# Sines before copies, one evacuation for the taps, and even-phase products kept in place, in a gated SSM and token-MLP kernel

## The chip, the cores and the metric

The kernel runs on one core of one Trainium2 chip. Its time is the device time of one execution, in microseconds (us). Six runs of the kernel before give a median of 189.79 us (188.96 to 190.0). One more execution was taken with the hardware profiler on; its own time was 191.53 us, of which 189.7 us are the span that the profile shows.

The engines are named as in the profile: PE is TensorE (PEld its weight loads), ACT is ScalarE, DVE is VectorE, POOL is GpSimd, and SP issues most of the DMAs. A `q` behind the name means that engine's queue.

## What is computed

Two branches share the input x = A_q (2048 x 640, bf16) and are mixed by a gate for each row. Branch A is a long convolution along the sequence, done by a Fourier transform in the reference. Branch B is an MLP over the sequence after a LayerNorm.

```python
g = sigmoid((x * gate_w).sum(-1, keepdims=True))
# A: k is shifted and weighted by 4 taps, multiplied by v, convolved with ssm_k
k_shift = sum over t of k_pad[:, t:t+S, :] * shift_k[:, 3 - t]
kv = k_shift * v
y = irfft(rfft(kv padded to 2S) * rfft(ssm_k padded to 2S))[:S] + kv * ssm_D
a = q * y
# B: MLP over the sequence axis
h = layernorm(x)
u = gelu(einsum("bsd,sf->bdf", h, w1) + b1)
b = transpose(einsum("bdf,fs->bds", u, w2) + b2)
out = g * a + (1 - g) * b
```

## The kernel before

**The planner.** The body of `_build` does not issue instructions directly. Each helper (`mms` for a group of matmuls, `act`, `tt`, `ts`, `dma`) adds an operation with an engine, a modelled duration, what it reads and writes, and a priority (by default its place in the text; `prio=0` is the most urgent). `_Sched.run` then plays a list schedule through: whenever an engine is free it takes, of the operations whose inputs are ready in the model, the one with the lowest priority number. The order that results is the program order of each engine, and the hardware waits are put in afterwards by `_Tracker` where data demand them. An `after` entry only orders two operations in the plan and makes no hardware wait. A DMA is modelled at 365 GB/s behind all earlier ones, plus 2 us. "QA" is the DMA queue of ScalarE, "SP" that of SyncE; `chain=True` keeps the SP loads in the order of the text.

**PSUM.** Four slots of 128 x 1024 f32. Groups of class "cv" (convolution branch and transposes) may hold three, "mlp" groups two. A group holds its slot from its first matmul to the end of its evacuation. The planner starts the matmuls of a group only when everything that its evacuation depends on is done.

**The stages.**
1. Small loads (D, shift taps, b2, b1), then ssm_k, x, w1, k, v on the SP queue.
2. Cosine and sine tables FTB, one of 1024 columns for each phase p. VectorE makes integer arguments `pint` (a product, an addition, a mask); ScalarE applies Sin. `pint` lies in the ring[1] buffer, which the k loads (`kn`) and one of the turned k buffers (`kp0`) use later. PORD = (0, 2, 1, 3) is the order of the phases.
3. `transp`: TensorE transposes ssm (five blocks db for each half h, eight matmuls each); ScalarE copies them to wT, which lies in C[2].
4. Taps. The loaded taps are rearranged by a VectorE copy ("taps") in `rows`, transposed by small matmuls ("cst"), and copied by ScalarE to `cw`. GpSimd spreads them to KF, which the products with k use as moving operand. `consts` does the same for b2 and b1 (cc).
5. `fwd(srcW(h), ...)`: for each half h and phase p four groups of four matmuls, 64 for each half, evacuated by ScalarE to C[h]. This is called W here. `mixing(C[0], SS, ...)` and `mixing(C[1], C[0], ...)` combine the phases on VectorE.
6. LayerNorm on VectorE (`ln_tile`, `ln_apply`), with the power on GpSimd (`ln_scale`), in two parts: tiles 0 to 7 are applied after the statistics of twelve tiles, the rest later. The first MLP product (m1, 384 matmuls, with a gelu for each of 12 blocks ft) needs the normalised X; its priority is so low that it fills TensorE's gaps.
7. `kv(hk)`: products of KT (k transposed by DMA) with KF, times v, for four blocks; blocks 0, 1 give vkv0 (source A), blocks 2, 3 give kv1 (source B).
8. `fwd_even` and `fwd` for A into C[2], for B into C[3]. Phases 1 and 3 are done by `fwd`, four groups each. Phases 0 and 2 share products: `fwd_even` makes eight groups of two matmuls, evacuates each to 640 columns of a temporary (Th, Ts) and forms slots 0 and 2 of the destination by three VectorE operations over them (two of 1280 columns and one of 2560, called the sums below). The temporary is slots 0 and 1 of C[1] for A and of C[2] for B. `mixing(C[1], C[0])` reads those slots of C[1] until its last operation, and `mixing(C[2], C[1])` those of C[2]. So phases 0 and 2 can be evacuated only after the mixing in question.
9. `mixing(C[2], C[1])`, `mixing_acc(C[3], ...)`, then the products in the spectrum (`cross`, `product`), partly summed by DMAs from GpSimd's queue, `invmix` and `inverse` for two halves, with ScalarE evacuating by the gate gg.
10. The second MLP product (m2, 384 matmuls, 16 groups), also filler, and the sum with branch A; the output is written in nine DMAs.

The gate's products (VectorE: X times gwb, 1280 columns, eight of them) and sums (ScalarE) are further filler between these.

All priorities of mixing C[0] and C[1] are MIXP = 330; the products of kv with v have priority 0.

The two lines that say where even-phase products go:

```python
act(V(Th, Ts * SL + D * pos[(p, kt, c)], [[320, 2], [1, 320]]), two, ACT.Copy, vt=vt, name="Ae")
fwd_even(srcA, 0, C[2], C[1], 0)
```

Of the kernel before, what the change touches and what calls it, by code (L numbers as in the profile page):

```python
# [323 lines left out]
class _Sched:  # L324
# [59 lines left out]
    def run(self):  # L384
# [12 lines left out]
        pend = {e: [] for e in engs}  # L397
        free = {e: 0.0 for e in engs}
        port = {"DVE": 0.0, "POOL": 0.0}
# [13 lines left out]
        n = len(ops)  # L413
# [97 lines left out]
def _build(nc, A_q, A_k, A_v, A_shift_k, A_ssm_k, A_ssm_D, B_x, B_w1, B_b1, B_w2, B_b2, gate_w, out):  # L511
# [10 lines left out]
    with ExitStack() as es:  # L522
# [27 lines left out]
        def base_of(h):  # L550
            return T.mem[h.name][1]
# [43 lines left out]
        ksh = [alloc(f"ksh{i}", [128, 4, D], BF16, at=base_of(GT) + 5120 * (1 + i)) for i in range(2)]  # L595
        rows = alloc("rows", [20, 4, 512], BF16, at=base_of(GT))
        kn = [alloc(f"kn{i}", [128, 4, D], BF16, at=base_of(ring[1]) + 5120 * i) for i in range(2)]
# [116 lines left out]
        def dr(t, off, ap):  # L714
            return bass.AP(tensor=t.tensor, offset=t.offset + off, ap=ap)
# [19 lines left out]
        def x_load(hk):  # L735
            dma(X[:, hk, :, :], dr(A_q, 512 * hk * D, [[4 * D, 128], [1, 4 * D]]), 128 * 5120, chain=True)
# [23 lines left out]
        def small(o, i, nbytes, stream, **kw):  # L760
            dma(o, i, nbytes, stream=stream, **kw)
# [3 lines left out]
        small(Drow[:, :], dr(A_ssm_D, 0, [[0, 1], [1, D]]), 1280, "QA")  # L765
        small(rows[0:20, 0, 0:128], dr(A_shift_k, 0, [[128, 20], [1, 128]]), 5120, "QA")
        small(rows[0:4, 1, :], dr(B_b2, 0, [[512, 4], [1, 512]]), 4096, "QA")
        small(rows[0:12, 2, 0:128], dr(B_b1, 0, [[128, 12], [1, 128]]), 3072, "QA")
        for a, b in SSM0:
            ssm_load(0, a, b)  # L770
        for hk in range(4):
            x_load(hk)
        for a, b in SSM1:
            ssm_load(1, a, b)
# [11 lines left out]
        ts("DVE", ident[:, :], dif[:, :], 0.0, None, ALU.is_equal)  # L786
        memset("POOL", cw[:, :, :], 0.0)
        ro, ri = rows[0:20, 3, :].rearrange("g (j q c) -> g j q c", j=4, q=4), V(rows, 0, [[1, 4], [0, 4], [4, 32]], pn=20)
        SC.add("DVE", 0.6, lambda s: T.op("DVE", lambda e: e.tensor_copy(ro, ri), [ri], [ro]), [ri], [ro], prio=0, name="taps")
        PORD = (0, 2, 1, 3)  # L790
        for p in PORD:
            pv = pint[:, p, :, 1, :]
            tt("DVE", pv, V(acol, p, [[4, 2], [0, 256]]), V(brow, 0, [[0, 2], [1, 256]]), ALU.mult, mode=1)
            ts("DVE", pint[:, p, :, 0, :], pv, 1024.0, None, ALU.add, mode=2)
            pa = pint[:, p, :, :, :].rearrange("q a b c -> q (a b c)")
            ts("DVE", pa, pa, 4095, None, ALU.bitwise_and, mode=2)
            act(FTB[:, p, :, :, :, :].rearrange("q a b c d -> q (a b c d)"), pa, ACT.Sin, bias=cst[:, 0:1],
                scale=-(2.0 * math.pi / 4096.0) * (1.0 - 1e-6), name="sin")
# [39 lines left out]

# [13 lines left out]

        def fwd_even(src, h, dst, Th, Ts):
# [9 lines left out]
            def t4(o, n, dims):  # L863
                return V(Th, Ts * SL + D * o, dims + [[1, n]])
            tt_("DVE", V(dst, 0, [[2 * D, 2], [1, D]]), t4(0, 2 * D, []), t4(2, 2 * D, []), ALU.add)
            tt_("DVE", V(dst, 2 * SL + 2 * D, [[-2 * D, 2], [1, D]]), t4(4, 2 * D, []), t4(6, 2 * D, []), ALU.add)
            tt_("DVE", V(dst, D, [[2 * SL, 2], [2 * D, 2], [1, D]]), t4(0, D, [[4 * D, 2], [D, 2]]), t4(2, D, [[4 * D, 2], [D, 2]]), ALU.subtract)

# [52 lines left out]
        for h in range(2):  # L921
            for db in range(ND):
                transp(h, db)
            if h == 0:
                consts()
            for p in PORD:
                fwd(srcW(h), h, p, C[h], p, 1.0 / 1024.0, "W", (lambda c, k2: False) if h == 0 else (lambda c, k2: c == 1))
            if h == 0:
# [14 lines left out]
                for g0 in KFP:  # L943
                    tt("POOL", KF[:, g0:g0 + 20 // len(KFP), :, :], V(cw, 7 * g0, [[7, 20 // len(KFP)], [1, 7], [0, 32]]), V(m32, 0, [[0, 20 // len(KFP)], [0, 7], [1, 32]]), ALU.mult)
                for hk in range(2):
# [313 lines left out]
```

## Time and profile before

| what | us |
|---|---|
| median of six runs | 189.79 |
| profiled execution, its own time | 191.53 |
| span of the profile | 189.7 |
| first transpose on TensorE | 3.93 |
| first wT copy on ScalarE | 5.04 |
| first W matmul on TensorE | 16.41 |
| last W evacuation, half 0 | 30.16 |
| mixing of C[1] begins on VectorE | 50.39 |
| mixing of C[2] begins on VectorE | 78.79 |
| first inverse begins on TensorE | 158.35 |
| second inverse begins on TensorE | 174.85 |
| last TensorE work ends | 187.04 |

Busy time by stage (us busy in each stretch):

| stretch | PE | DVE | ACT | POOL |
|---|---|---|---|---|
| 0 to 6 | 1.54 | 5.00 | 2.24 | 1.21 |
| 6 to 16.4 | 5.42 | 9.60 | 10.27 | 5.77 |
| 16.4 to 30.2 | 13.79 | 11.21 | 10.36 | 5.69 |
| 30.2 to 50.4 | 19.29 | 16.37 | 18.03 | 14.85 |
| 50.4 to 66.4 | 15.95 | 15.53 | 14.20 | 2.67 |
| 66.4 to 78.8 | 12.30 | 7.48 | 12.40 | 2.43 |
| 78.8 to 98.6 | 18.62 | 19.47 | 18.78 | 0.89 |
| 98.6 to 158.2 | 59.60 | 59.37 | 17.85 | 12.28 |
| 158.2 to 174.8 | 15.59 | 12.99 | 9.00 | 4.80 |
| 174.8 to 189.7 | 12.20 | 11.69 | 6.34 | 0.00 |

A busy TensorE is not TensorE at its best: matmuls are pipelined, and a slow one counts as busy all the while. In a line of a timeline the columns are: start, length, engine, line of the code, operation, destination and source with their shapes, number of instructions merged, and in brackets the idle time before and what ended it. In the chain of waits the columns are start, length and what the chain ran through. Most operations carry the line of a helper (L667 for every ACT evacuation, L623 for every two-input VectorE operation, L293 for every matmul), so the names of the tiles tell them apart; buffer numbers are left out, so "C" is any of C[0] to C[3].

### The profile page before, as it was taken

What the parts mean: (1) busy time and instruction counts of PE and PEld (TensorE: products, weight loads), DVE (VectorE), ACT (ScalarE), POOL (GpSimd) and SP (SyncE); (2) the same over time, 40 slices, a digit from 0 to 9 for tenths busy, and PEclk for the clock granted to TensorE, in tenths of its full rate; (3) what the DMA queues carried; (4) which work ended last, traced back from release to release, by engine and by line L of the source; (5) the groups of instructions that cost most, each with busy time, mean ns of one, the idle gap of its engine ahead of it and who ended that gap; (6) DMA issues with size and microseconds to landing.
All of it is one profiled execution on the core that took longest, in us unless ns stands there. A gap on an engine that the chain in (4) does not pass through costs nothing.

```text
span 189.7 us, 3316 instructions
## 1 busy us (share of the span) xinstructions
PE 174.3 (92%) x1374; PEld 130.1 (69%) x1374; DVE 168.7 (89%) x199; ACT 119.5 (63%) x180; POOL 50.6 (27%) x41
## 2 busy tenths in 40 slices
PE   2746999989999999999979999999999999997994
PEld 1523668756877786767747777888888887675673
DVE  7899795999399963999999999999999999849984
ACT  2996789699997999999798111322313134553660
POOL 2079404999000550000011530200205050342000
PEclk9999999999999999999999999999999999999999
DMA  5999999899990799990799699957949999999453
GB/s 173 377 412 369 386 199 238 345 416 207 200 352 24 182 211 230 232 202 0 137 222 271 108 192 159 340 98 211 313 90 284 271 190 243 275 196 226 105 207 138
DMA packets 38206, 42.85 MB, mean 226 GB/s; under 512 B 15787, under 2 KB 31280, under 8 KB 38192
## 3 DMA queue, kind: packets, MB, share of 16 engines
q1 hardware_dynamic: 33200, 32.15, 56.9%
q0 software_dynamic: 4928, 10.49, 31.1%
q8 instruction: 10, 0.16, 0.3%
q14 instruction: 4, 0.03, 0.1%
q10 hardware_dynamic: 64, 0.01, 0.0%
HBM read 25.87 MB, written 2.62 MB: 150 GB/s over the span
## 4 chain that ended last, share of the span: by engine, by line
PE 80%; ACT 15%; DMA 2%; issue 1%; DVE 0%
PE pp L293 80%; ACT C L667 4%; ACT wT L667 3%; ACT FTB L667 3%; ACT ksh L667 2%; DMA ssm<-in_A_ssm_k_dram 2%; ACT L667 1%; ACT GT L667 1%; ACT O L667 0%; ACT cw L667 0%; DVE O L679 0%; ACT gth L667 0%
## 5 line engine op out<-in xcount | busy, mean ns | idle before, releaser
L623 DVE TENSOR_TENSOR C<-C 128x2560 bf16<-128x2560 bf16 (+2 forms) x34 | 52.2, 1564 | 7.3 <-ACT C L667 7.2
L293 PE MATMUL pp<-X,ring 128*128 128x320 bf16 x384 | 55.4, 299 | 1.5 <-ACT GT L667 1.2
L293 PE MATMUL pp<-GT,W 128*128 128x320 bf16 x384 | 52.8, 299 | 0.0
L293 PEld LDWEIGHTS pp<-GT,W 128*128 128x128 bf16 x384 | 43.4, 113 | 8.9 <-ACT cgb L667 0.2
L293 PEld LDWEIGHTS pp<-X,ring 128*128 128x128 bf16 x384 | 37.2, 98 | 16.5 <-issue 1.9
L667 ACT ACTIVATE C<-pp 128x640 bf16<-128x640 f32 x64 | 40.5, 717 | 6.5 <-PE pp L293 6.4
L667 ACT ACTIVATE O<-pp,c,omg 128x640 bf16<-128x640 f32 x15 | 13.3, 885 | 34.7 <-PE pp L293 34.7
L293 PE MATMUL pp<-wT,FTB 128*128 128x320 bf16 x128 | 21.8, 329 | 2.2 <-ACT wT L667 1.4
L262 POOL DMA_DIRECT2D C<-q_hi x6 | 5.9, 984 | 54.5 <-DVE C L623 27.6
L293 PEld LDWEIGHTS pp<-wT,FTB 128*128 128x128 bf16 x128 | 13.0, 107 | 9.8 <-ACT wT L667 1.5
L262 POOL DMA_DIRECT2D C<-C x8 | 9.9, 1360 | 34.0 <-DVE C L623 33.8
L667 ACT ACTIVATE GT<-pp,cc 128x640 bf16<-128x640 f32 x12 | 9.5, 791 | 13.1 <-PE pp L293 12.9
L667 ACT ACTIVATE cgb<-pp,gg 128x640 bf16<-128x640 f32 x16 | 12.7, 793 | 6.9 <-PE pp L293 5.4
L293 PE MATMUL pp<-C,FTB 128*128 128x320 bf16 x96 | 13.6, 299 | 1.1 <-ACT O L667 1.1
L996 POOL COPY KT<-KT 128x20 bf16<-128x20 bf16 x1 | 14.0, 13956 | 2.3 <-DMA KT<-kp 2.3
L623 DVE TENSOR_TENSOR tm<-C,C 128x2560 bf16<-128x2560 bf16 (+1 forms) x7 | 14.4, 2057 | 0.0
L899 DVE BATCH_NORM_STATS2 stats<-X 128x6 f32<-128x320 bf16 x32 | 13.4, 461 | 0.8 <-DMA X<-in_A_q_dram 0.8
L623 DVE TENSOR_TENSOR SS<-C 128x2560 bf16<-128x2560 bf16 x8 | 11.6, 1486 | 2.0 <-DMA C<-C 1.8
L293 PEld LDWEIGHTS pp<-C,FTB 128*128 128x128 bf16 x96 | 8.9, 98 | 5.4 <-ACT O L667 1.6
L623 DVE TENSOR_TENSOR C<-tm 128x2560 bf16<-128x2560 bf16 (+1 forms) x10 | 12.0, 1219 | 0.0
L667 ACT ACTIVATE gq<-gq 128x640 bf16<-128x640 bf16 x16 | 11.8, 748 | 0.0
L293 PE MATMUL pp<-ident,ssm 128*128 128x128 bf16 x80 | 8.4, 270 | 3.7 <-DMA ssm<-in_A_ssm_k_dram 2.6
(69 smaller groups left out, 192.9 us busy)
## 6 DMA issues: line engine op xcount, KB each, us to landing
ring<-in_B_w_dram SPq DMA_DIRECT2D x12, 512.0 KB, 11.0
W<-in_B_w_dram SPq DMA_DIRECT2D x8, 768.0 KB, 7.2
C<-C POOLq DMA_DIRECT2D x8, 640.0 KB, 10.7
X<-in_A_q_dram SPq DMA_DIRECT2D x4, 640.0 KB, 8.5
kn<-in_A_k_dram SPq DMA_DIRECT2D x4, 640.0 KB, 8.4
out_dram<-O SPq DMA_DIRECT2D x7, 320.0 KB, 2.8
ssm<-in_A_ssm_k_dram SPq DMA_DIRECT2D x3, 512.0 KB, 5.8
vkv<-in_A_v_dram SPq DMA_DIRECT2D x2, 640.0 KB, 5.0
```

What stands on the lines that cost most here:

```text
L262: ins = engobj.dma_start(out_ap, in_ap, accum_op=ALU.add, max_dma_last_dim=2560)
L293: ins = self.nc.tensor.matmul(ps_ap, lhsT=lhsT, rhs=rhs, start=start, stop=stop, skip_group_check=True)
L623: o_ = SC.add(eng, d, lambda s: T.op(eng, lambda e: e.tensor_tensor(o, a, b, op), [a, b], [o]), [a, b], [o], prio=prio, name="tt")
L667: return T.op("ACT", lambda e: e.activation(o, src, func, **kw), rr + [src], ww)
L899: ops.append(SC.add("DVE", 0.38, (lambda o, i: lambda s: T.op("DVE", lambda e: e.bn_stats(o, i), [i], [o]))(o, i), [i], [o]))
L996: SC.add("POOL", 0.3, lambda s: T.op("POOL", lambda e: e.tensor_copy(KT[1][:, :, 15:16], KT[0][:, :, 143:144]), [KT[0][:, :, 143:144]], [K ...
```

## The change

1. The planner takes ScalarE as busy until 2.0 us. The argument chains of the four phases are kept in order one behind the other. The copy of wT block 0 may only follow the sine of phase 0 in the plan, the copies of blocks 1 to 4 that of phase 2. The sines of phases 1 and 3 get priorities a little ahead of the W groups of phase 0 and of phase 1.
2. The taps are laid out so that each of four groups of 32 partitions gets its own shift by the layout itself: seven small transposes fill 140 columns, and one evacuation of 128 x 140 writes all of `cw`, zeros included. Before, it was four transposes and four evacuations of 32 x 80, onto a `cw` that was set to zero. `rows` gets a fifth row, and GpSimd zeroes `rows` instead of `cw`.
3. The loads of the shift taps, b2 and b1 move from ScalarE's DMA queue to SP's: the taps behind the second ssm load, b2 and b1 behind the x loads. D stays.
4. `fwd_even` evacuates its eight products to slots 1 and 3 of the destination itself, and the sums read them there. Phases 1 and 3 are written to the same slots afterwards.
5. The two mask operations for m32 get priority 0, and KF may only follow the last argument chain in the plan.

```diff
-        free = {e: 0.0 for e in engs}
+        free = {e: 2.0 if e == "ACT" else 0.0 for e in engs}
...
-        rows = alloc("rows", [20, 4, 512], BF16, at=base_of(GT))
+        rows = alloc("rows", [20, 5, 512], BF16, at=base_of(GT))
...
-        small(rows[0:20, 0, 0:128], dr(A_shift_k, 0, [[128, 20], [1, 128]]), 5120, "QA")
-        small(rows[0:4, 1, :], dr(B_b2, 0, [[512, 4], [1, 512]]), 4096, "QA")
-        small(rows[0:12, 2, 0:128], dr(B_b1, 0, [[128, 12], [1, 128]]), 3072, "QA")
-        for a, b in SSM0:
+        for a, b in SSM0[:2]:
+            ssm_load(0, a, b)
+        small(rows[0:20, 0, 0:128], dr(A_shift_k, 0, [[128, 20], [1, 128]]), 5120, "SP", chain=True)
+        for a, b in SSM0[2:]:
             ssm_load(0, a, b)
         for hk in range(4):
             x_load(hk)
+        small(rows[0:4, 1, :], dr(B_b2, 0, [[512, 4], [1, 512]]), 4096, "SP", chain=True)
+        small(rows[0:12, 2, 0:128], dr(B_b1, 0, [[128, 12], [1, 128]]), 3072, "SP", chain=True)
...
-        memset("POOL", cw[:, :, :], 0.0)
-        ro, ri = rows[0:20, 3, :].rearrange("g (j q c) -> g j q c", j=4, q=4), V(rows, 0, [[1, 4], [0, 4], [4, 32]], pn=20)
+        memset("POOL", rows[0:20, 3:5, :].rearrange("g a b -> g (a b)")[:, 0:896], 0.0)
+        ro, ri = V(rows, 1536, [[128, 4], [160, 4], [1, 32]], pn=20), V(rows, 0, [[1, 4], [0, 4], [4, 32]], pn=20)
...
+        sins = {}
         for p in PORD:
             pv = pint[:, p, :, 1, :]
-            tt("DVE", pv, V(acol, p, [[4, 2], [0, 256]]), V(brow, 0, [[0, 2], [1, 256]]), ALU.mult, mode=1)
+            t_ = tt("DVE", pv, V(acol, p, [[4, 2], [0, 256]]), V(brow, 0, [[0, 2], [1, 256]]), ALU.mult, mode=1)
...
-            ts("DVE", pa, pa, 4095, None, ALU.bitwise_and, mode=2)
-            act(FTB[:, p, :, :, :, :].rearrange("q a b c d -> q (a b c d)"), pa, ACT.Sin, bias=cst[:, 0:1],
+            if p != 0:
+                t_.after.add(pprev)
+            pprev = ts("DVE", pa, pa, 4095, None, ALU.bitwise_and, mode=2)
+            sins[p] = act(FTB[:, p, :, :, :, :].rearrange("q a b c d -> q (a b c d)"), pa, ACT.Sin, bias=cst[:, 0:1],
                 scale=-(2.0 * math.pi / 4096.0) * (1.0 - 1e-6), name="sin")
...
-        for j in range(4):
-            items.append(((lambda s, j=j: s[:, 512 + 20 * j:512 + 20 * j + 20]), rows[0:20, 3, 128 * j:128 * j + 128], ident[0:20, 0:20], True, True))
+        for j in range(7):
+            items.append(((lambda s, j=j: s[:, 512 + 20 * j:512 + 20 * j + 20]), V(rows, 1536 + 128 * j, [[1, 128]], pn=20), ident[0:20, 0:20], True, True))
         mms(vt, items, prio=0, name="cst")
-        for q in range(4):
-            act(V(cw, q, [[7, NG], [1, 4]], p0=32 * q, pn=32), (lambda s, q=q: s[32 * q:32 * q + 32, 512:592].rearrange("p (j g) -> p g j", j=4)), ACT.Copy, vt=vt, prio=0, name="cw")
+        act(cw[:, :, :], (lambda s: s[:, 512:652].rearrange("p (j g) -> p g j", j=7)), ACT.Copy, vt=vt, prio=0, name="cw")
...
-        ts("DVE", dif2[:, :], dif2[:, :], 31, None, ALU.bitwise_and, mode=2)
-        ts("DVE", m32[:, :], dif2[:, :], 0.0, None, ALU.is_equal, mode=2)
+        ts("DVE", dif2[:, :], dif2[:, :], 31, None, ALU.bitwise_and, mode=2, prio=0)
+        ts("DVE", m32[:, :], dif2[:, :], 0.0, None, ALU.is_equal, mode=2, prio=0)
...
-            act(V(wT, 2 * h * SL + 128 * db, [[SL, 2], [D, 4], [1, 128]]), (lambda s: s[:, :].rearrange("q (a b c) -> q a b c", a=2, b=4)), ACT.Copy, vt=vt, name="wT")
+            o_ = act(V(wT, 2 * h * SL + 128 * db, [[SL, 2], [D, 4], [1, 128]]), (lambda s: s[:, :].rearrange("q (a b c) -> q a b c", a=2, b=4)), ACT.Copy, vt=vt, name="wT")
+            if h == 0:
+                o_.after.add(sins[0 if db == 0 else 2])
...
-                        act(V(Th, Ts * SL + D * pos[(p, kt, c)], [[320, 2], [1, 320]]), two, ACT.Copy, vt=vt, name="Ae")
+                        act(V(dst, SL * (1 + p) + D * (pos[(p, kt, c)] % 4), [[320, 2], [1, 320]]), two, ACT.Copy, vt=vt, name="Ae")
...
             for p in PORD:
+                if h == 0 and p in (1, 3):
+                    sins[p].prio = SC.ops[-1].idx - (16.5 if p == 1 else 8.5)
                 fwd(srcW(h), h, p, C[h], p, 1.0 / 1024.0, "W", (lambda c, k2: False) if h == 0 else (lambda c, k2: c == 1))
...
-        fwd_even(srcA, 0, C[2], C[1], 0)
+        fwd_even(srcA, 0, C[2])
...
-        fwd_even(srcB, 1, C[3], C[2], 0)
+        fwd_even(srcB, 1, C[3])
```

The sums read slots 1 and 3 of the destination in the same pairs as before, with the same three shapes.

More of the change, by code (lines that the diff above doesn't have):

```diff
@@ L851, in fwd, with fwd_even @@
                     act(o, two, ACT.Copy, vt=vt, name=name + "e", **kw)
-        def fwd_even(src, h, dst, Th, Ts):
+        def fwd_even(src, h, dst):
             pos = {(0, 0, 0): 0, (0, 0, 1): 1, (0, 1, 0): 2, (0, 1, 1): 3, (2, 0, 1): 4, (2, 1, 0): 5, (2, 1, 1): 6, (2, 0, 0): 7}
@@ L860, in fwd_even @@
                         mms(vt, items, name="A")
-                        act(V(Th, Ts * SL + D * pos[(p, kt, c)], [[320, 2], [1, 320]]), two, ACT.Copy, vt=vt, name="Ae")
[L863 to L867, printed above, removed]
+                        act(V(dst, SL * (1 + p) + D * (pos[(p, kt, c)] % 4), [[320, 2], [1, 320]]), two, ACT.Copy, vt=vt, name="Ae")
+            tt_("DVE", V(dst, 0, [[2 * D, 2], [1, D]]), V(dst, SL, [[D, 2], [1, D]]), V(dst, SL + 2 * D, [[D, 2], [1, D]]), ALU.add)
+            tt_("DVE", V(dst, 2 * SL + 2 * D, [[-2 * D, 2], [1, D]]), V(dst, 3 * SL, [[D, 2], [1, D]]), V(dst, 3 * SL + 2 * D, [[D, 2], [1, D]]), ALU.add)
+            tt_("DVE", V(dst, D, [[2 * SL, 2], [2 * D, 2], [1, D]]), V(dst, SL, [[2 * SL, 2], [D, 2], [1, D]]), V(dst, SL + 2 * D, [[2 * SL, 2], [D, 2], [1, D]]), ALU.subtract)
         def mixing(R, Th, Ts, fine=False, conj=False, prio=None):
@@ L943, in _build @@
                 for g0 in KFP:
-                    tt("POOL", KF[:, g0:g0 + 20 // len(KFP), :, :], V(cw, 7 * g0, [[7, 20 // len(KFP)], [1, 7], [0, 32]]), V(m32, 0, [[0, 20 // len(KFP)], [0, 7], [1, 32]]), ALU.mult)
+                    k_ = tt("POOL", KF[:, g0:g0 + 20 // len(KFP), :, :], V(cw, 7 * g0, [[7, 20 // len(KFP)], [1, 7], [0, 32]]), V(m32, 0, [[0, 20 // len(KFP)], [0, 7], [1, 32]]), ALU.mult)
+                    k_.after.add(pprev)
                 for hk in range(2):
```

## The prediction

> **What bounds the kernel now.** I read the engine shares first, then the chain that ended last in order of time, then the timelines of ScalarE, VectorE and TensorE around the places where that chain leaves TensorE. The shares:
>
> ```profile
> PE 174.3 (92%) x1374; PEld 130.1 (69%) x1374; DVE 168.7 (89%) x199; ACT 119.5 (63%) x180; POOL 50.6 (27%) x41
> ```
>
> Two engines are nearly full, so both have to finish sooner before the end can move. The start of the chain of waits shows where neither of them leads:
>
> ```profile
> 0.72 3.16 DMA ssm<-in_A_ssm_k_dram
> ...
> 6.08 1.28 ACT L667
> 7.37 0.01 issue
> 7.38 2.19 ACT FTB L667 x2
> 9.57 0.13 ACT cw L667
> ...
> 10.51 1.02 ACT wT L667
> 11.54 2.08 ACT FTB L667 x2
> 13.61 2.75 ACT wT L667 x3
> 16.36 0.05 issue
> 16.41 11.84 PE pp L293 x64
> ```
>
> From 5.04 to 16.36 us ScalarE works without a gap: a copy of wT, a table load, two sines (FTB), four cw copies, wT, two sines, wT three times. Only then can TensorE begin the first spectral products (W, half 0). Their pace, from the timeline of ScalarE:
>
> ```profile
> 20.89 0.70 ACT L667 ACTIVATE C<-pp 128x640 bf16<-128x640 f32 x1 [0.36 <-PE pp L293]
> 21.96 5.66 ACT L667 ACTIVATE C<-pp 128x640 bf16<-128x640 f32 x9 [0.36 <-PE pp L293]
> ```
>
> Up to 21 us an eviction waits for TensorE and the pitch is 1.07 us; afterwards it is 5.66/9 = 0.63 us and ScalarE is the slower one. Later, the waits that matter on VectorE and the last one on TensorE, from their timelines:
>
> ```profile
> 50.39 2.83 DVE L623 TENSOR_TENSOR C<-C 128x5120 bf16<-128x5120 bf16 x1 [3.10 <-ACT C L667]
> ...
> 72.84 0.83 DVE L623 TENSOR_TENSOR C<-C 128x1280 bf16<-128x1280 bf16 x1 [2.57 <-ACT C L667]
> ...
> 75.24 2.23 DVE L623 TENSOR_TENSOR C<-C 128x1280 bf16<-128x1280 bf16 x2 [1.58 <-ACT C L667]
> ...
> 174.85 4.54 PE L293 MATMUL pp<-C,FTB 128*128 128x320 bf16 x32 [1.05 <-ACT O L667]
> ```
>
> The reader should see four things: VectorE starts the mixing of C[1] 3.10 us late because half 1 of W is late; it waits 2.57 and 1.58 us for the even-phase products of A; from about 78.8 to 158.2 us it has no gap worth naming (19.47 of 19.80 and 59.37 of 59.60 us busy in two windows); and at the end TensorE waits 1.05 us where the second inverse begins just as VectorE's Z1 appears (173.22 + 1.49 us). The end is thus a tie of both engines, TensorE with about 1 us in hand.
>
> **What the Trainium skill says.** (1) "ScalarE: Activation LUTs", What ACT_TABLE_LOAD costs: about 1283 ns a load. The trace has three loads of mean 1283 ns and no more between load and sine. Same page, Table sets: copy is in every set. The trace agrees: copies follow the sines at 9.48 us without a load. So a start with a sine needs one load where copy, sine needs two. (2) "TensorE: Matmul & The Clock Gate", Part 1: the array runs at half rate until it was busy for a window of some 3.4 us. The pitch of 1.07 us, then 0.63 us, for four 128x320 matmuls agrees. (3) "DMA: Bandwidth & Descriptors", HWDGE ordering: each engine takes a queue's descriptors in ring order[...]. No run of before shows this for small loads.
>
> **The change, part by part.**
>
> *Table and sines.* The first ScalarE work becomes the sine of phase 0. VectorE has its argument at about 3.5 us: ident to 1.55, then 0.65 multiply, 0.35 for the two mask operations now pulled forward, 0.41 and 0.69. The one load runs at about 1.3 us instead of 2.31 (three of four DMA issues, 0.97 us, left this queue). Sine 0 then lies in 3.6 to 4.7 us, ahead of wT 0, which TensorE releases at 5.04 as before. Removed from ScalarE's stretch from 5.04: one load 1.28, sine 0 1.09, and sines 1 and 3 (2.18), which go behind the wT copies.
>
> *Taps.* Four cw copies of 0.25 us pitch become one of 128x140. Between the rows 128x28 (0.215) and 128x512 (0.610) the slope is 0.82 ns a column, so 0.31 us: 0.7 saved. Seven tiny matmuls for four: four took 0.27, seven at most 0.47. The GpSimd fill of rows (896 columns) replaces that of cw (140 columns, 0.21): 0.2, or 1.3 if it grows with the columns; GpSimd is idle from 1.86 to 10.63 and the taps copy comes at about 5.9, so nothing.
>
> *Small loads.* Three issues of 0.31 to 0.33 us move to SP. Past the first: ssm 3:5, all X loads; past all three: ssm of half 1 and w1, about 1.0 us later issued. SP issued 768 KB by 1.7 us of which 584 KB had moved by 4 us, so the rings have backlog and landings don't move. The shift taps now land with ssm 1:3, for which TensorE waited until 6.23: 6.3 to 6.5 us. VectorE reaches the taps copy at about 5.9, so it stalls about 0.6 (0 to 1.5), and the last phase's argument is ready at 9.5 instead of 8.2; statistics start at 9.5 instead of 9.10. b2 and b1 land behind X at some 13.5 us; their matmuls are in the planned order by modelled landing, so behind the first W groups, and cost nothing unless they land after 16.
>
> *Where W starts.* ScalarE alone would be done 5.3 us earlier, but TensorE's transposes now bind: ssm 1:3 at 6.23, four groups of 1.22 us pitch, tap matmuls 0.45 and slot waits 0.2 to 0.5 give 11.6, wT 4 of 1.0 gives 12.6. I take 12.5 (11.9 to 13.3) for 16.41: 3.9 us gained.
>
> *The postponed sines.* Sine 1 fits where ScalarE waits for the first W group; sine 3 stands ahead of phase 1. W half 0 is then 16 x 0.63 + 1.1 us on ScalarE from 13.6, to 24.8 if TensorE is at full rate, about 25.7 if it spends four groups at half rate; before it ended at 30.16. k loads reuse pint, and SP waited for sine 1 until 12.67; it now waits until about 13.7. The copy that needs them is at 23.29 on VectorE with a landing of 8.4 us: covered, unless sine 1 slides past 15.
>
> *LayerNorm.* Its twelve first tiles end at 20.06 (19.66 + 0.4). GpSimd's KF (8.14 us) starts when cw is there, at 9.3 for 10.63, so rstd is out at 19.4 and the wait of 1.13 us goes: net 0.7 gained. The second wait for rstd (2.12) stays. VectorE runs to 46.5 instead of 47.3, then finds W half 1 complete if it moved the 3.9 us (50.36 to 46.5): it starts mixing C[1] 3.8 us earlier.
>
> *Even products in place.* No instruction is saved. Before, they went to C[1] and had to wait until mixing C[1] was read through (66.4), so the odd phases ran first (58.8 to 65.5) and the sums came at 72.84 to 77.47. Now even phases run first, into slots 1 and 3 of C[2], beside mixing C[1]; the three sums (0.82 + 0.82 + 1.49) follow at once, at 66.4 on the old clock. New wait: odd evictions into those slots wait for the sums; eight groups of 0.65 and a first matmul make 5.8 us. Mixing C[2] can start at 69.5 + 5.8 = 75.3 instead of 78.79: 3.5 gained, at best 4.9 if all idle time of that window goes, nothing if the filling work (five gate products of 0.82, two kv products of 1.49) is badly placed. I take 2.5. For half B the cross products of 0.82 and 1.49 us hide the same wait.
>
> *Sum.* VectorE: 3.8 + 2.5 = 6.3. TensorE: 3.9 from the start; its loss of 3.0 in W (52 matmuls of 0.136 in 10.03 us) becomes 1.7 to 2.7, so 0.8; the 1.2 us before 98.59 (a slot held by evictions to C[2]) likely half, 0.6; and the 1.05 at the end goes as VectorE leads. That is 6.3 too. From a tie of two sums I subtract 1.5 for orders that the new list of work places worse, as neither can be read off this trace: 4.8. The span of 189.7 becomes 184.9; the profiled execution (191.53, 1.83 around the span) would be 186.7. The median 189.79 lies 1.74 under that execution, so I forecast 185.0.
>
> **Rivals.**
> *Front only* (186.4 to 188.3): the start gains 3.9, but VectorE, bound by LayerNorm until 33, passes on only part, and the odd wait eats the even gain. For it: VectorE at 89%. Against: 3.10 + 2.57 + 1.58 us of its idle time have ScalarE as releaser. Worked: 0.7 + half of 3.1 = 2.2, so 187.6.
> *More* (181.5 to 183.2): dense transposes from 6.23 to 11.6 bring TensorE to full rate before W, 1.0 us more, and no order is worse, 1.5 more: 182.5. For it: the gaps of 1.12 and 1.79 between transposes go. Against: the same transposes ran at half rate up to 12.9, and the window's phase is not in view.
> *No gain* (within 0.6): the gain at the start is taken by later work, 189.8.
> *Slower, the odd phases wait* : place, between the sums and the mixing of C[2] and C[3]. Price 5.8 us for each half, 11.6 together, if VectorE has nothing else ready; against it 4.9 of idle time removed and 3.8 from the front: 2.9 lost, 192.7. It decides from where the sums of A end later than 73.0 us on the old clock (78.79 - 5.8) plus the 3.8 of the front, and B does likewise. For it: kv products stand at priority 0, ahead of the sums. Against: all filling work together, 2.98 + 4.1 us, delays them by 7.1 from 66.4 and so barely to 76.6.
>
> **How the numbers follow.** Chances: forecast (183.2 to 186.4) 0.52, front only 0.23, more 0.12, no gain 0.05, slower 0.08. The range 182.0 to 188.0 leaves out a part of "more", the tail of "front only" and the last two cases, some 0.2. What can't be told from no change is 0.3%, 0.6 us: faster 0.87, same 0.05, slower 0.08.
>
> **What would show it.** Two table loads, the first before 2 us, and a sine ahead of any wT; one cw of about 0.3 us; first W matmul near 12.5; the 3.10 before mixing C[1] under 1; waits of 2.57 and 1.58 replaced by less than 2 together; mixing C[2] starting about 6 us earlier; TensorE's 1.05 near 175 gone. Wrong would be a long wait of VectorE or TensorE for the rows load near 6 us, W after 14, or VectorE idle over 4 us between the sums of A and mixing C[2].

## The result, and the profile after

The changed kernel is about as slow as the one before: ratio 1.0038, 95% interval 1.0018 to 1.0058. The forecast was 185.0 us, 2.5% faster. The ratio leaves out every execution more than 1.5% above the fastest of its kernel, which are 18 of this kernel's 32 and 2 of before's 67; over all of them the medians are 192.17 us (189.06 to 199.28) and 190.0 us (188.96 to 192.43), 1.1% apart. The profiled execution took 190.57 us, with a span of 188.5. That is 1.2 us shorter than the span of before, but before's profiled execution (191.53 us) lies 1.5 us above the median of its kernel and this one 1.6 us below that of its own. The profiles are therefore read for places, not for that difference.

The shares, as before in the first line of the page:

```profile
PE 174.6 (93%) x1377; PEld 128.6 (68%) x1377; DVE 171.6 (91%) x199; ACT 118.1 (63%) x176; POOL 38.4 (20%) x41
```

VectorE is busy 2.9 us longer than before with 199 instructions in both. The chain that ended last (start, length, what it ran through) says where:

```profile
2.58 8.00 DMA X<-in_A_q_dram
10.58 0.02 issue
10.60 0.49 DVE stats L903
11.10 1.40 DVE pint L637
12.49 0.40 DVE stats L903
12.89 2.07 DVE pint L637
...
84.75 4.28 ACT C L667 x7
...
91.78 4.31 ACT gq L667 x12
96.09 0.03 ACT GT L667
96.12 17.40 DMA GTB<-FTB x2
```

Before, this chain began with ScalarE's tables and copies. Now it begins with VectorE, and from 84.73 to 115.66 us it runs outside TensorE: 11.4 us on ScalarE, through evacuations and the sums of the gate (gq), then 19.5 us through the transposes of the tables (GTB<-FTB) and what waits for them. Two places have to be explained. The first, from VectorE's timeline and from GpSimd's:

```profile
10.60 0.49 DVE L903 BATCH_NORM_STATS2 stats<-X 128x6 f32<-128x320 bf16 x1 [2.50 <-DMA X<-in_A_q_dram]
11.01 1.48 DVE L637 TENSOR_SCALAR pint<-pint 128x512 int32<-128x512 int32 x1
12.41 0.48 DVE L903 BATCH_NORM_STATS2 stats<-X 128x6 f32<-128x320 bf16 x1
12.81 2.15 DVE L637 TENSOR_SCALAR pint<-pint 128x1024 int32<-128x1024 int32 x1
...
24.57 2.18 DVE L638 TENSOR_SCALAR X<-X,mv,rstd 128x640 bf16<-128x640 bf16 x6
...
53.21 7.17 DVE L623 TENSOR_TENSOR C<-C 128x5120 bf16<-128x5120 bf16 x4
```

```profile
8.12 8.76 POOL L623 TENSOR_TENSOR KF<-cw,m 128x1120 bf16<-128x1120 bf16 x4 [5.33 <-ACT cw L667]
```

The same work in the kernel before, where KF starts at 10.63 us and so behind all arguments:

```profile
5.53 0.41 DVE L637 TENSOR_SCALAR pint<-pint 128x512 int32<-128x512 int32 x1
7.51 0.70 DVE L637 TENSOR_SCALAR pint<-pint 128x1024 int32<-128x1024 int32 x1
9.10 1.28 DVE L899 BATCH_NORM_STATS2 stats<-X 128x6 f32<-128x320 bf16 x3 [0.80 <-DMA X<-in_A_q_dram]
20.79 2.58 DVE L638 TENSOR_SCALAR X<-X,mv,rstd 128x640 bf16<-128x640 bf16 x7 [1.13 <-POOL rstd L623]
```

Now VectorE idles 2.50 us for X, because one statistics instruction stands ahead of the last two argument instructions; and these two, an addition and a mask that took 0.41 and 0.70 us before, take 1.48 and 2.15 beside GpSimd's products for KF. The application of the norm starts at 24.57 us (20.79 before), the mixing of C[1] at 53.21 (50.39). The wait of 3.10 us ahead of that mixing is gone, yet it begins later.

The second place, in the timelines of TensorE, ScalarE and SyncE:

```profile
12.32 5.04 PE L293 MATMUL pp<-wT,FTB 128*128 128x320 bf16 x23 [0.77 <-ACT wT L667]
...
109.08 4.52 PE L293 MATMUL pp<-X,ring 128*128 128x320 bf16 x32 [0.97 <-ACT GT L667]
115.66 40.37 PE L293 MATMUL pp<-GT,W 128*128 128x320 bf16 x296 [2.06 <-ACT GT L667]
...
171.45 4.54 PE L293 MATMUL pp<-C,FTB 128*128 128x320 bf16 x32
```

```profile
107.04 1.35 ACT L667 ACTIVATE FTB<-GTB 128x1024 bf16<-128x1024 bf16 x1 [6.11 <-DMA GTB<-FTB]
108.26 0.77 ACT L667 ACTIVATE GT<-pp,cc 128x640 bf16<-128x640 f32 x1
```

```profile
92.98 1.42 SPq L267 DMA_DIRECT2D W<-in_B_w_dram  x2
96.12 15.28 SPq L260 DMA_TRANSPOSE GTB<-FTB  x4
```

The start of W on TensorE at 12.32 us (a single matmul of it ran at 11.10) and the lost wait at 171.45 are as forecast. But TensorE now stands 0.97 and 2.06 us for a gelu (GT), where it stood 1.18 us in the kernel before:

```profile
98.59 17.55 PE L293 MATMUL pp<-X,ring 128*128 128x320 bf16 x128 [1.18 <-ACT GT L667]
```

The gelu was held on ScalarE: a copy that interleaves the transposed tables (FTB<-GTB) stands ahead of it in the order and waits 6.11 us for its transpose. In the kernel before, the same queue of SyncE and the first summing transfer of this part on GpSimd's read:

```profile
80.70 13.61 SPq L260 DMA_TRANSPOSE GTB<-FTB  x4
94.35 21.09 SPq L267 DMA_DIRECT2D W<-in_B_w_dram  x4
```

```profile
96.08 0.89 POOL L262 DMA_DIRECT2D C<-q_hi  x1 [26.95 <-DVE c L623]
```

These four DMAs transpose the tables for the inverse, a phase each, into GTB, and four ScalarE copies interleave the result back into FTB. Before, they were as good as over when the loads of the second MLP matrix (W) and the summing transfers began, and landed 3.0 to 4.8 us after issue. Now two loads are issued ahead of them, and sums run beside them, issued at 92.73, 96.58, 100.89 and 104.83 us; the transposes land after 4.1 to 10.9 us. In the view of GTB, before and after:

```profile
DMA to landing us min/median/max: 3.0/3.2/4.8
```

```profile
DMA to landing us min/median/max: 4.1/8.0/10.9
```

They are issued late because GTB's place holds gate products until these are summed; in the chain above ScalarE's gate sums run up to the first transpose. Five of the eight gate products used to come before the mixing of C[2], several in VectorE's gaps; with the gaps gone, two lie there and six behind, the last at 94.73 us (88.53 before).

### The profile page after: what moved, and what is told of

Same layout as the page of the kernel before. It is cut to its first block, busy times and chain, and to the rows that moved or that the text cites. A ratio compares the mean times of both kernels' runs of the same rounds, so it can differ in the third digit from the quotient of the medians.

```text
span 188.5 us, 3317 instructions
## 1 busy us (share of the span) xinstructions
PE 174.6 (93%) x1377; PEld 128.6 (68%) x1377; DVE 171.6 (91%) x199; ACT 118.1 (63%) x176; POOL 38.4 (20%) x41
## 3 DMA queue, kind: packets, MB, share of 16 engines
HBM read 25.87 MB, written 2.62 MB: 151 GB/s over the span
## 4 chain that ended last, share of the span: by engine, by line
PE 66%; DMA 13%; ACT 10%; DVE 8%; SPq 1%; issue 1%
PE pp L293 66%; DMA GTB<-FTB 9%; DVE stats L903 5%; DMA X<-in_A_q_dram 4%; ACT C L667 4%; ACT gq L667 3%; DVE pint L637 2%; ACT GT L667 1%; SPq L267 1%; ACT FTB L667 1%; ACT L667 1%; DVE mv L905 1%; DVE O L679 0%; DVE X L638 0%
## 5 line engine op out<-in xcount | busy, mean ns | idle before, releaser
L293 PEld LDWEIGHTS pp<-wT,FTB 128*128 128x128 bf16 x128 | 12.0, 103 | 11.2 <-ACT C L667 4.0
L623 DVE TENSOR_TENSOR SS<-C 128x2560 bf16<-128x2560 bf16 x8 | 11.6, 1484 | 2.0 <-DMA C<-C 2.0
L667 ACT ACTIVATE FTB<-GTB 128x1024 bf16<-128x1024 bf16 x4 | 5.4, 1356 | 9.3 <-DMA GTB<-FTB 9.3
L667 ACT ACTIVATE wT<-pp 128x1024 bf16<-128x1024 f32 x10 | 9.7, 1029 | 2.4 <-PE pp L293 2.4
(69 smaller groups left out, 188.5 us busy)
```

The source lines that it names most:

```text
L293: ins = self.nc.tensor.matmul(ps_ap, lhsT=lhsT, rhs=rhs, start=start, stop=stop, skip_group_check=True)
L623: o_ = SC.add(eng, d, lambda s: T.op(eng, lambda e: e.tensor_tensor(o, a, b, op), [a, b], [o]), [a, b], [o], prio=prio, name="tt")
L667: return T.op("ACT", lambda e: e.activation(o, src, func, **kw), rr + [src], ww)
```

## Experiments

All ratios are to the kernel before, on the same chip.

**The two halves.** The front alone (even phases as before; the body of `fwd_even` goes back with them):

```diff
-        fwd_even(srcA, 0, C[2])
-        fwd_even(srcB, 1, C[3])
+        fwd_even(srcA, 0, C[2], C[1], 0)
+        fwd_even(srcB, 1, C[3], C[2], 0)
```

> The changed kernel with the even products back in C[1] and C[2]: the front part alone. If the even part is what starves the gate products (VectorE has no idle time for them any more): transposes start by 85, no gelu wait of TensorE, time a little under the kernel before (0 to 1%), as VectorE's early loss of 3.8 us eats the start. If the front alone moves the gate products: transposes after 92 and gelu waits as in the changed kernel.

The kernel before with only the even phases in place (the reverse of this diff):

> The kernel before with only the even products in place. If the even part gains what the prediction said (2.5 us on VectorE) and late gate products do not cost: 1% under the kernel before. If it starves the gate products: transposes after 92, gelu waits, time equal to or above the kernel before.

The front alone: 1.0031 (0.9995 to 1.0068). The even phases alone: 1.065 (1.0611 to 1.0689). Neither half gives a gain. The second costs the most: its transposes are issued from 96.09 us on and land after up to 19.6 us, ScalarE waits 15.8 us for them and TensorE 10.0 for gelus, besides 2.8 for a load of W. In the front alone they land after 3.0 to 3.2 us and nothing waits for them. Why both halves together lose less than the second alone was not tested; SyncE's order differs (two loads ahead of all transposes in the changed kernel, one ahead and one between them here).

**VectorE's start.** The first statistics are planned behind the last argument instruction, and KF is held until that has run:

```diff
-                    ln_tile(t // 4, t % 4)
+                    for o_ in ln_tile(t // 4, t % 4):
+                        o_.after.add(pprev)
...
+                    kr = [ka, kb_, pint[:, 3, 0, 0, :]]
```

On the changed kernel:

> The changed kernel, but no LayerNorm statistics before the last argument chain in the plan, and KF really waits for that chain. Theory A (one statistics operation got ahead of the last argument pieces, waited in order for X, and the pieces then ran beside KF at 1.48 and 2.15 us instead of 0.43 and 0.69): pieces back at 0.43 and 0.69, first apply of X near 21.5 instead of 24.57, VectorE some 3 us earlier as far as the second inverse; time 0.5 to 1.5% lower, limited by TensorE's gelu waits. Theory C (late landing of X is what matters): apply no earlier than 23.5, time the same.

On the front alone:

> The change's front part alone (even phases as before), with the first statistics placed behind the last argument instruction in VectorE's order and the taps' products on GpSimd held until the last arguments are made. Theory (the front's gain on TensorE of 4 us was eaten by VectorE starting its LayerNorm 3.8 us later): the application of the norm starts at about 21 us (24.6 in the changed kernel) and the ratio to before falls from the 1.003 of the front part alone to 0.98 to 0.99. Rival (the front gives nothing because VectorE and the transfers bound the first 70 us anyway): ratio 0.995 to 1.005 in spite of the earlier norm.

In the changed kernel the start was mended as expected (norm applied from 20.95 us), but the time rose to 1.0481 (1.0424 to 1.0538), a miss: the transposes now land after up to 22.0 us, and TensorE stands for a gelu 10.6 us at a stretch. Why they land still later was not tested; the sums beside them are closer together (issued at 93.27 and 95.23 us instead of 92.73 and 96.58). On the front alone the same edit gives 0.9902 (0.9873 to 0.9932). Its timeline of VectorE:

```profile
7.93 1.16 DVE L637 TENSOR_SCALAR pint<-pint 128x512 int32<-128x512 int32 x2
9.83 1.28 DVE L905 BATCH_NORM_STATS2 stats<-X 128x6 f32<-128x320 bf16 x3 [0.74 <-DMA X<-in_A_q_dram]
20.31 2.17 DVE L638 TENSOR_SCALAR X<-X,mv,rstd 128x640 bf16<-128x640 bf16 x6
```

Both argument instructions together take 1.16 us instead of 1.04 and 2.15 in the front alone, and the norm is applied 4.4 us earlier (24.74 there). So the start of VectorE is what ate the front's gain, 1.3% (1.0031 - 0.9902); the new plan also moves some later work on ScalarE and TensorE, and the runs don't price that apart. The small loads are the rival cause. Put back on ScalarE's queue in the changed kernel:

```diff
-        small(rows[0:20, 0, 0:128], dr(A_shift_k, 0, [[128, 20], [1, 128]]), 5120, "SP", chain=True)
+        small(rows[0:20, 0, 0:128], dr(A_shift_k, 0, [[128, 20], [1, 128]]), 5120, "QA")
```

(b2 and b1 likewise.)

> The changed kernel with the taps, b2 and b1 loads back on ScalarE's queue. Theory C (these three loads delay X by 1.5 us and with it VectorE): first X lands near 9.1 instead of 10.6, first apply 1.5 us earlier, time 0.5% or more lower; but the table load and the first sine move back by about 1 us. Theory A: the last argument pieces still run beside KF, first apply at 23 or later, time within 0.5%.

X was there by 8.87 us instead of 10.60. All profiles bear this out: the first statistics, which wait for X in each of them, start at 9.83 to 11.52 us in the ten kernels with the moved loads and at 8.87 to 9.80 us in the ten others. So moving the loads does delay X; but the argument instructions still took 1.86 and 2.14 us beside KF, the norm came only 1.4 us earlier (23.21), and the ratio is 1.006 (1.002 to 1.01): no gain.

**The gelus.** The interleaving copies are planned behind the last gelu:

```diff
-... ACT.Copy, prio=10 ** 5, name="gil")
+... ACT.Copy, prio=10 ** 5, name="gil").after.add(glast)
```

> The changed kernel, but in the plan the four interleaving copies (FTB from GTB) come after the last gelu; nothing else moves on any other engine. Theory B (these copies wait for late transposes in ScalarE's order and hold back gelus, so TensorE loses 0.97 + 2.06 us): both waits of TensorE vanish, fewer m2 matmuls stand behind the second inverse (about 20 instead of 40), end 2 us earlier, up to the bound that VectorE sets; time about 1 to 1.5% under the changed kernel. Theory A alone (only VectorE's early delay counts): no change within 0.3%.

With the start mended as well:

> Both edits of the two runs before together. Theories A and B together: the sum, 4 to 5 us under the changed kernel, about 186 us, below the kernel before. If only one of them is right: the same as that one's run.

Alone: 0.9971 (0.9947 to 0.9995), with TensorE's two waits for gelus gone; 0.7% of the changed kernel's time was lost there, less than the 1 to 1.5% expected. With the start mended: 1.0272 (1.0213 to 1.0332), a miss. The transposes still land late (8.2 to 19.4 us), and the wait moved from the gelus to the evacuations of the second MLP product, which now queue behind the copies (TensorE waits 4.63 us for one). So the order on ScalarE only says who pays for late transposes.

**Why they land late.** First, gate products ahead of other VectorE work, so that transposes can be issued sooner:

```diff
-... V(gwb, 0, [[0, 2], [1, D]]), ALU.mult)
+... V(gwb, 0, [[0, 2], [1, D]]), ALU.mult, prio=330.5)
```

> The changed kernel, with the VectorE gate products at a priority just behind mixing C[0] and C[1], so that the last three come before the sums of B instead of after; the order before mixing C[2] is unchanged. Theory D (late gate products hold the transposes of FTB into the same buffer back, so that these meet the summing DMAs and land late, and the interleaving copies then hold gelus): transposes start near 84 us instead of 96, land in 3 to 5 us instead of 8, TensorE's gelu waits near 109 and 115 under 0.5 us together; time 1 to 2% under the changed kernel. Theory E (the transposes are slow wherever they stand): waits stay near 3 us, time the same.

A miss: 1.0833 (1.0761 to 1.0905). Two transposes went at 88.06 and 89.97 us and landed in about 3 us; the other two went from 91.97 on, just as the sums began, and landed after up to 28.7.

Three edits of the kernel with only the even phases in place were then meant to tell sums from loads:

> The kernel before with the even phases in place, and every summing transfer of the even phase and of the last inverses' products turned into a plain copy of the same bytes on the same queue: the additions of these transfers are left out, so the output isn't the reference's; the order on every engine is unchanged. Theory A (a transpose beside a transfer that sums lands late because that transfer sums, i.e. [...]holds the engines longer): the four transposes land in 3 to 5 us (3.9/10.9/19.6 with summing), ScalarE waits under 3 us for them instead of 15.8, ratio to before about 1.00. Rival B (any transfer of GpSimd's queue does it): transposes stay at a median over 8 us, ratio stays at 1.05 to 1.07. Rival W (the loads of the second matrix on SyncE's queue do it): as B.

> The same kernel with these summing transfers left out altogether (their additions are left out, so the output isn't the reference's). Theory A and rival B: transposes land in 3 to 5 us, ScalarE waits under 3 us for them, ratio to before below 1.00 (0.97 to 1.00, since the inverses also lose a wait). Rival W: the transposes still land at a median over 8 us and ScalarE still waits 8 us or more.

> The same kernel with its sums kept, but all loads of the second matrix of the MLP issued only after the last transpose was issued. Rival W: transposes land in 3 to 5 us, ScalarE waits under 3 us for them, ratio to before about 1.00. Theory A and rival B: the median stays over 8 us or the longest over 10 us, ScalarE still waits 8 us or more for them, and the loads now come late on top: ratio 1.05 to 1.09.

They gave 1.057 (1.0501 to 1.0639), 1.0555 (1.0497 to 1.0613) and 1.0756 (1.069 to 1.0821), with longest landings of 19.2, 19.8 and 21.8 us, and decided nothing: the transfers changed in the first two lie behind the transposes (from 123 us on), and the third held the loads behind only the transpose that is issued first. They serve as repeats of the 19.6. The edits were made again at the right places, in `mixing_acc` and `cross`, and for all four transposes:

```diff
-                dma(pr(R, i), pr(R, 2 + i), 128 * 5120, stream="POOL", prio=0, accum=True)
+                dma(pr(R, i), pr(R, 2 + i), 128 * 5120, stream="POOL", prio=0)
...
-                dma(comp(V1[g], i, 0), tmp, 128 * 5120, stream="POOL", prio=0, accum=True)
+                dma(comp(V1[g], i, 0), tmp, 128 * 5120, stream="POOL", prio=0)
```

> The kernel before with the even phases in place, and the six summing transfers that GpSimd's queue issues between 90 and 109 us (two of the last mixing, four of the products) turned into plain copies of the same bytes on the same queue: their additions are left out, so the output isn't the reference's; the order on every engine is unchanged. Theory A (a transpose beside a transfer that sums lands late because that transfer sums): the transposes land in 3 to 6 us at the most of the four (3.9/10.9/19.6 with summing), ScalarE waits under 5 us for them instead of 15.8, ratio to before 1.00 to 1.02. Rival B (any transfer of GpSimd's queue does it) and rival W (the loads of the second MLP matrix, issued ahead of and between the transposes, do it): longest landing over 12 us, ratio 1.05 to 1.07.

(without the two lines:)

> The same kernel with these six transfers left out (their additions are left out, so the output isn't the reference's). Theory A and rival B: longest landing under 6 us, ScalarE waits under 5 us for them, ratio to before at most 1.02. Rival W: longest landing over 12 us and ScalarE waits over 10 us all the same.

```diff
+                w2last.after.update(tps)
```

> The same kernel with its six sums kept, but every load of the second MLP matrix behind all four transposes in SyncE's order. Rival W: longest landing under 6 us, ScalarE waits under 5 us for the transposes, ratio to before at most 1.02. Theory A and rival B: the longest landing stays over 10 us; ScalarE still waits 8 us or more.

> Both: the six sums left out (the output isn't the reference's) and the loads behind the transposes. Every theory of a collision: the transposes land in 3.0 to 3.6 us each, as in the kernel before; ScalarE's wait for them falls under 5 us. If they land late here too, neither of the two kinds of transfer is the cause, and what holds them is on the transposes' own side (their source or the gate products' buffers).

The landings, from issue, of the four transposes, in the view of this tile: first with the even phases alone, then with plain copies, with the loads behind, and with the loads behind and no sums. ScalarE waits 15.8, 2.2 and 6.4 us for them in the first three, and not at all in the last.

```profile
DMA to landing us min/median/max: 3.9/10.9/19.6
```

```profile
DMA to landing us min/median/max: 5.1/7.2/10.7
```

```profile
DMA to landing us min/median/max: 6.7/6.8/8.5
```

```profile
DMA to landing us min/median/max: 3.1/3.2/3.3
```

Without the sums but with the loads it is 3.2/4.9/6.3. Neither theory holds alone: loads ahead make 3.3 into 6.3, sums beside make it 8.5, and only both together make 19.6. The sums slow the loads too. Of the two loads around the transposes the slower lands after 20.1 us with sums, 8.2 with plain copies, 6.2 with neither; that a transpose behind such a load on the same queue waits with it fits these figures, and no run shows it alone. The Trainium skill ("DMA: Bandwidth & Descriptors", Queues, rings and completion order) says that a DMA engine goes round its queues packet by packet; that fits the step from 3.3 to 8.5 with sums alone. That a sum weighs more there than a copy of the same bytes is what the plain copies show (10.7 against 19.6). The view of the DMA queues from 88 to 122 us has the size of it, for GpSimd's queue (packets, MB, share of the 16 engines), with sums and with plain copies:

```profile
q0 software_dynamic: 1120, 2.62, 45.9%
```

```profile
q0 software_dynamic: 608, 2.62, 22.9%
```

The same bytes go in nearly twice as many packets, and these take twice the engines' time; why sums are cut into more packets is open.

The plain copies are also the proof for the time, since every engine keeps its order: the ratio falls from 1.065 to 0.998 (0.9958 to 1.0001), and TensorE's waits for gelus from 10.0 to 1.2 us. These transfers leave out their additions and land sooner for VectorE too, but that engine's order and work are the same, and in the profile with sums it waits for none of them. Where sums are left out or loads moved back, VectorE's and TensorE's later orders differ, and the times (1.0114, 1.0167 and 1.0242, two runs each) say little.

The loads behind all transposes in the changed kernel itself:

> The changed kernel with the loads of the second MLP matrix behind all four transposes in SyncE's order; TensorE's order is unchanged, in ScalarE's and VectorE's orders a few instructions near the transposes change places. Theory (sums and loads together held the transposes): longest landing 6 to 9 us instead of 10.9, ScalarE waits about 4 to 6 us for them instead of 9.3, ratio to before 0.995 to 1.002, below the changed kernel's 1.0038. Rival (the 3.0 us that TensorE loses to the gelus come from ScalarE's order alone): TensorE's waits for the gelus stay at 3 us and the ratio at 1.004.

Landing 4.7 to 7.5 us, ScalarE's wait 5.0 us instead of 9.3, TensorE's 3.0 us for gelus gone; but the loads, now later, keep TensorE waiting 1.30 and 1.10 us, and the ratio is 1.0032 (1.0012 to 1.0052), above the 0.995 to 1.002 expected and no different from the changed kernel's 1.0038: one wait for another.

**All edits of order together** (start, copies behind gelus, gate products sooner), without and with the loads behind:

> All four edits: arguments ahead of statistics, KF behind the arguments, gate products early, interleaving copies behind the last gelu. Theories A and D: VectorE 3 us earlier at the apply of X, transposes from about 82 us in 3 to 5 us each, no TensorE wait over 1 us between 60 and 165; 184.5 to 186.5 us, below both kernels. If the collision of the transposes stays (E), 190 or more.

> The kernel with the four edits of order (statistics, taps' products, interleaving copies, gate products) and the loads of the second MLP matrix behind all four transposes; only SyncE's order differs from the one without that. Nothing waits for the transposes there any more, so the theory expects no gain: transposes land in 3 to 6 us, ratio to before 0.982 to 0.989 as without it. Rival (the loads, now later, come too late for the second matmul of the MLP): ratio above 0.99, with TensorE waiting for W at about 115 us.

0.985 (0.9811 to 0.9888), median 186.98 us, and 0.984 (0.9808 to 0.9872), median 186.9: faster than both kernels. From the first, SyncE's and TensorE's timelines:

```profile
80.10 6.27 SPq L260 DMA_TRANSPOSE GTB<-FTB  x2
87.22 0.40 SPq L267 DMA_DIRECT2D W<-in_B_w_dram  x1
87.68 4.14 SPq L260 DMA_TRANSPOSE GTB<-FTB  x2
```

```profile
99.79 11.30 PE L293 MATMUL pp<-X,ring 128*128 128x320 bf16 x82
110.93 9.26 PE L293 MATMUL pp<-GT,W 128*128 128x320 bf16 x67
```

The last transpose is issued at 89.0 us, the first sum at 90.77; the longest landing is 7.4 us and nobody waits for one. TensorE goes from the first MLP product to the second without a gap. The gate products' priority is the only edit between the 1.0272 above and this 0.985. It cost 8% when it stood alone and is right here, since with the earlier start it brings all four transposes, not two, ahead of the sums. Whether the even products in place add to the gain is not shown: the front with its start mended has 0.9902, and the two intervals overlap.

## Why the prediction was wrong, point by point

Two steps failed: "net 0.7 gained" at the LayerNorm, and "nothing" as the least that the even products in place could gain. Every sign that the prediction lists under "What would show it" came true all the same: none of them looks at VectorE from 9 to 25 us, or at the transposes and gelus between 90 and 116 us.

- *Table and sines, taps*: right. Sine 0 began at 3.43 us (forecast 3.6), `cw` took 0.29 us (0.31).
- *Where W starts*: 12.32 us (12.5), in part by luck. The second group of transposes ran at 5.13 us and not at 6.23, but the fourth stood 1.08 us for a late ssm load, until 8.90; and the sum given as 11.6 leaves out the slot waits of 0.2 to 0.5 that it names. W's first half was evacuated by 25.42 us (24.8 to 25.7).
- *Small loads*: "landings don't move", "statistics start at 9.5 instead of 9.10". Wrong. X arrived at 10.58 us, with one statistics instruction ahead of the last arguments, which I had not looked for; the rows load cost next to nothing.
- *LayerNorm*: "net 0.7 gained". This step failed. I let KF start sooner on an idle GpSimd and charged it to nobody. The order that the change asks for, KF behind the last arguments, holds in the plan alone: KF started at 8.12 us, and nothing on the chip made it wait. The two argument instructions took 3.63 us instead of 1.11, and with the 2.50 us for X the norm came 3.8 us late instead of 0.7 early. The Trainium skill has it ("SBUF — State Buffer", Who interferes with whom): a VectorE `tensor_scalar` can need a port pair that a GpSimd instruction holds to its end, one with a single input in the plain mode doesn't. The trace agrees: in six profiles the addition ends 0.27 to 0.28 us after the piece of KF in which it started (GpSimd makes KF in four), whether that makes it 0.55 or 1.86 us long, while the statistics beside KF kept 0.48 us. The runs with order and KF mended together put the price at 1.3% of the time; they don't part the two.
- *Even products in place*: the mechanism was right, the sum missed its other side. Waits of 2.57 and 1.58 us are gone; the mixing of C[2] began at 71.59 us, 7.2 earlier (about 6 forecast) in spite of the late start. But I bounded this edit at "nothing" from below. The gaps it closed had been housing gate products, and the transposes hang on these. VectorE's stretch from there to the first inverse grew from 79.6 to 84.3 us, and late transposes and loads cost 6.7% with the even phases alone (1.065 against 0.998).
- *Sum*: the 1.5 us for "orders that the new list places worse" was the term for this, and far too small: the best order gains 1.5% (2.8 us), and the change's own order gives all of that and 0.4% more away, 1.9% or some 3.6 us together. Of the wait of TensorE before 98.59 us half, 0.6, was to go; in its place came 0.97 and 2.06. And even the best order has 2.8 of the 6.3 us that stand before the 1.5 is taken off; where the rest went the runs don't show.
- *Rivals*: "no gain" had the number and a chance of 0.05, but named no place for the loss. The odd phases' wait, my case for slower, did not come. The case that did, a transfer that the change lets run into other transfers, was not among them.
- TensorE's last wait went as forecast, but 40 matmuls of the second MLP product instead of 24 stood behind the second inverse, so of the 3.4 us by which that came earlier in the two profiles 1.3 are left when TensorE ends.

## What to carry to other kernels

Before closing an engine's gaps, list the filler in them and what hangs on it: the work does not vanish, and a transfer at its end may move into traffic. When a list of work is planned anew, compare every queue's order, those of DMAs first; here one instruction on VectorE, GpSimd's start, and the place of four copies and eight gate products, which moved four transposes on SyncE, made the difference between 0.4% slower and 1.5% faster. An order that stands in the plan alone is no order on the chip. An instruction started sooner on an idle engine is free only if what runs beside it on the others keeps its duration.

## What was not expected of the hardware

- A DMA transpose of one phase's table lands in 3.1 to 3.3 us with neither sums nor loads near it, in 6.7 to 8.5 beside summing transfers, and in up to 19.6 (28.7 in one kernel) with loads ahead of it in its queue as well.
- Six summing transfers of GpSimd's queue took 1120 packets for 2.62 MB, plain copies of the same bytes 608.
- A 768 KB load took 20.1 us beside sums against 8.2 beside plain copies of the same bytes.
- A VectorE instruction of 0.41 us took 0.55 to 1.86 us beside GpSimd's products over 1120 columns, depending on how much of a product was left when it started; one of 0.70 took 2.14 to 2.15.
- A long stop of TensorE is paid again afterwards. In the changed kernel with the start mended, TensorE's timeline and the row of its granted clock (tenths, in 40 slices of 4.9 us):

```profile
89.41 17.55 PE L293 MATMUL pp<-X,ring 128*128 128x320 bf16 x128
117.59 6.18 PE L293 MATMUL pp<-X,ring 128*128 128x320 bf16 x32 [10.63 <-ACT GT L667]
```

```profile
PEclk9999999999999999999999756999999999999999
```

After 10.63 us of waiting, 32 matmuls took 6.18 us; before the stop 128 took 17.55, or 4.39 for 32. The Trainium skill ("TensorE: Matmul & The Clock Gate", Part 1) has the clock fall back to half after an idle window of some 3.4 us, and this agrees: the granted clock is 7, 5 and 6 tenths in the three slices from 108 to 123 us and 9 in all others. An estimate from the page's window, half rate from 3.4 us after the stop began (106.96 us) to 3.4 us after it ended, gives 0.74, 0.50 and 0.67 for them.
